# Another order of the seven products in the first two gate/up units, one of them in a down-product bank

## The chip, the cores and the metric

The kernel runs on 1 core of one Trainium2 chip. The metric is the device time of one execution in microseconds (us); where a program runs several times, the median is given. The engines are named as in the profile: PE (TensorE, matmuls), PEld (its weight loads), DVE (VectorE), ACT (ScalarE), POOL (GpSimd), SP (SyncE, which here issues DMA transfers; SPq is its queue).

## What is computed

All in float32; S = 2048 rows, D = 576 columns, F = 4608 hidden columns, 32 heads:

```python
x = A_x
xn = _layernorm(x)
s = _A_ref(xn, ...)                 # attention with a learned feature map
g = _silu((_silu(xn @ w_gate) * (xn @ w_up)) @ w_down)
return x + s * g
```

The change lies in `_silu(xn @ w_gate) * (xn @ w_up)` alone, the gate/up part of the FFN, and in the order in which its inputs are loaded.

## The kernel before

**Precision.** Every float32 operand of a matmul is split in two parts: a high part (ACT, a cast) and the rest (DVE, a subtraction); both stand on lines 58 and 59, in the helper `split`. A product is the sum of three such matmuls per block.

**The FFN in units.** The hidden columns are worked in 36 blocks of 128 (`NF`), and the rows in two halves `i` of 1024. A pair (half, block) is a unit. The first five blocks (`EARLY`) were computed ahead, beside the attention, and are only loaded again in the FFN (`stored`). For the other units `gate_up` makes, from the weights of one block, two tiles of 128 by 512 for gate and two for up, by a scheme with seven products in place of eight (`product`, L702 to L706). A product is seven matmuls of 512 columns: six on the main rows and one on the tail rows (`wt`). The seven are numbered by the weight block that they use, the third argument of `product`: 0 with the input A11, 4 with S1, 1 with A12, 5 with S2, 2 with S3, 6 with A22, 3 with S4. S1 to S4 are sums of input blocks that were stored in DRAM (`sum_dram`); the A blocks are the input itself.

**Banks.** Product results pile up in PSUM. Bank `px` (two copies) takes products 0, 5, 2 and 6 one after the other, and between them ACT copies its state out: to bank `py` after 0 (L747), to `s2` after 5 and to `s3` after 2 (`snap`, L735). Bank `py` takes product 1 on top and gets the silu in place (L751). Bank `pw` takes 4 and 3. DVE adds `pw` to `s3` (L740, `add`), multiplies it with the silu of `px` (L761) to the tile `hb` (L762), and, after product 3, adds `pw` to `s2` and multiplies with `py` to the tile `ha` (L766). The down products have banks of their own, `pd` (two of them, each over two banks of PSUM).

**The weights of a unit.** `gate_up_weights` loads a block (`ld`), POOL makes differences (`ts`, and parts of `ld`, L693 to L696), and ACT and DVE split them into tiles `w` of two blocks each, for products 0 and 1, 4 and 5, 2 and 3, and a single one for 6. There are four of the double tiles and two of the single ones: a new tile takes over one whose products are done. In the first half the split weights are also stored (`w_dram`).

**The down products.** `strassen` queues the products of two pairs of units with the down weights. Its operands are prepared by POOL (differences, L889 to L907), ACT and DVE (splits, tiles `hh` from `ha`, `hb` and `h`, and `dw` from the down weights; the first rows of these lie in `acc`). `fill` takes finished items from the queue and puts their matmuls (L805) between the products of a later unit. The queue is empty during the first two gate/up units; the third is the first that finds something in it. A list scheduler then places every instruction of every engine by its operands and priorities, so a product's matmuls may be placed among those of another unit.

**The order of the loads.** `operands(i)` issues from SP the loads of the inputs of a half in a written order, L650: A11, S1, A12, S2, S3, A22, S4. In the second half all seven are loaded, each into the tile of the first half, so that a load waits for the last product of the first half that reads that tile. The queue of SP is strictly in order.

Of the kernel before, what the change touches and what calls it, by code (L numbers as in the profile page):

```python
# [9 lines left out]
F32 = mybir.dt.float32  # L10
F32R = mybir.dt.float32r
AF = mybir.ActivationFunctionType
# [5 lines left out]
P = 128  # L18
# [4 lines left out]
NF = F // P  # L23
# [6 lines left out]
EARLY = 5  # L30
# [16 lines left out]
def gated_hedgehog_kernel(ctx: ExitStack, tc, x, w_qk, w_v, w_phi, wo, w_gu, w_tail, w_down, ident_in, mask_in, out):  # L47
# [5 lines left out]
    nc = tc.nc  # L53
# [17 lines left out]
    h_dram = dram.tile([2, EARLY, P, HS], F32, name="h_dram")  # L71
# [54 lines left out]
    with ExitStack() as att:  # L126
# [364 lines left out]
        with ExitStack():  # L491
# [5 lines left out]
            for i in range(3):  # L497
                for j in range(4 if i < 2 else 2):
                    w = GROUPS[(4 * i + j) // 2][1]
                    nc.scalar.copy(zc[0:w, 4 * i + j:4 * i + j + 1], kvp[i][0:w, j, w:w + 1])  # L500
            for s in range(2):
                for a, m, name in ((0, 4, ("p2", "vw")[s]), (4, 1, ("vy", "vx")[s])):
                    o, w = GROUPS[a]
                    zp = kps.tile([P, 512], F32, name=name)
# [5 lines left out]
            for i in range(2 * NG):  # L510
                o, w = GROUPS[i // 2]
# [135 lines left out]
    def operands(i):  # L647

        xo = [None] * 7
        for n in (0, 6, 1, 3, 5, 2, 4):  # L650
            if n < 3:
                j = (0, 1, 3)[n]
                if i:
                    t = xpool.tile([P, 5, BT], F32R, name=f"X0{j}")
                    nc.sync.dma_start(t.bitcast(F32), a_dram[n])
                else:
                    t = XB[0][j]
                xo[n] = [t[:, c] for c in range(5)]
                continue
            j = n - 3  # L660
            t = xpool.tile([P, 5, BT], F32R, name=f"X1{j}")
            nc.sync.dma_start(t.bitcast(F32).rearrange("p c n -> p (c n)"),
                              sum_dram[i, :, j].rearrange("p s c n -> p (s c n)"))
            v = t.rearrange("p c n -> p (c n)").rearrange("p (s c n) -> p s c n", s=4, c=5)
            xo[n] = [v[:, :, c] for c in range(5)]
        return xo

    def gate_up_weights(i, f):

        parts, wt = {}, fw.tile([96, 7, P], F32R, name="wt", bufs=2)  # L670
        n, q = divmod(f - EARLY, 4)
        if i == 0:
            ld = fw.tile([P, 2, D], F32, name="ld", bufs=2).rearrange("p a b -> p (a b)")
            ld = ld[:, 0:8 * P].rearrange("p (m c n) -> p m c n", m=4, c=2)
            nc.sync.dma_start(ld, w_gu[f, :, :, 0:2])
            ts = fw.tile([P, D], F32, name="ts")[:, 0:4 * P].rearrange("p (m c n) -> p m c n", m=2, c=2)

        def ready(m, src):
            k = 1 if m == 6 else 2
            w = fw.tile([P, k, 4, P], F32R, name=f"w{k}", bufs=2 if k == 1 else 4)  # L680
            if i:
                nc.sync.dma_start(w.bitcast(F32), w_dram[f - EARLY, :, m:m + k])
            else:
                split(w[:, :, 0:2], w[:, :, 2:4], src)
                if f < NF - 1:
                    nc.sync.dma_start(w_dram[f - EARLY, :, m:m + k], w.bitcast(F32))
            for c in range(k):
                parts[m + c] = w[:, c]

        ready(0, None if i else ld[:, 0:2])  # L690
        nc.sync.dma_start(wt.bitcast(F32), t_dram[n, q].rearrange("b r m n -> (b r) m n"))
        if i == 0:
            nc.gpsimd.tensor_sub(ts[:, 0], ld[:, 2], ld[:, 0])  # L693
            nc.gpsimd.tensor_sub(ts[:, 1], ld[:, 3], ts[:, 0])
            nc.gpsimd.tensor_sub(ld[:, 2], ld[:, 3], ld[:, 2])
            nc.gpsimd.tensor_sub(ld[:, 1], ld[:, 1], ts[:, 1])  # L696
        ready(4, None if i else ts)
        ready(2, None if i else ld[:, 2:4])
        ready(6, None if i else ld[:, 1:2])
        return parts, wt  # L700

    def product(ps, w, m, b, first, last):  # L702
        mm = [(w[0][m][:, i], b[j]) for c in range(2) for i, j in ((c, c), (2 + c, c), (c, 3 + c))]
        mm += [(w[1][:, m], b[2][0:96])]
        for n, (l, r) in enumerate(mm):
            nc.tensor.matmul(ps, l, r, start=first and n == 0, stop=last and n == len(mm) - 1, skip_group_check=True)  # L706

    def short(name, bufs):
        return fq.tile([P, BT], F32, name=name, bufs=bufs)

    def h_tile():
        return [fp.tile([P, BT], F32, name=n, bufs=b) for n, b in (("ha", 7), ("hb", 6))]
# [6 lines left out]
    def stored(src, fill):  # L719
        h = h_tile()  # L720
        for r in range(2):
            nc.sync.dma_start(h[r], src[:, r * BT:(r + 1) * BT])
        for _ in range(2):
            fill()
        return h

    def gate_up(w, xo, fill, opening):
        A11, A12, A22, S2, S4, S3, S1 = xo
        xp, yp, wp = (fps.tile([P, BT], F32, name=n, bufs=b) for n, b in (("px", 2), ("py", 1), ("pw", 1)))
        h = h_tile()  # L730

        def snap(ps):
            t = short("s", 3)
            with tc.high_priority():
                nc.scalar.copy(t, ps)  # L735
            return t

        def add(ps, t):
            with tc.high_priority():
                nc.vector.tensor_add(t, ps, t)  # L740


        if opening:
            nc.tensor.matmul(yp, w[0][0][:, 0], A11[0], start=True, stop=True)
        product(xp, w, 0, A11, True, False)
        with tc.high_priority():
            nc.scalar.copy(yp, xp)  # L747
        product(wp, w, 4, S1, True, False)
        fill()
        product(yp, w, 1, A12, False, True)  # L750
        nc.scalar.activation(yp, yp, AF.Silu)  # L751
        product(xp, w, 5, S2, False, False)
        s2 = snap(xp)
        fill()
        product(xp, w, 2, S3, False, False)
        s3 = snap(xp)
        add(wp, s3)
        fill()
        product(xp, w, 6, A22, False, True)
        with tc.high_priority():  # L760
            nc.scalar.activation(xp, xp, AF.Silu)  # L761
        nc.vector.tensor_mul(h[1], xp, s3)  # L762
        product(wp, w, 3, S4, False, True)
        add(wp, s2)
        with tc.high_priority():
            anchor.append(nc.vector.tensor_mul(h[0], yp, s2))  # L766
        fill()
        return h

# [200 lines left out]
    queue, anchor, share = [], [], [2]  # L970

    def look():
        n = 0
        for step in queue:
            n += step[0]
            if n > 4 or (step is not queue[0] and step[0] == 1 and n > 3):
                break
            if step[1]:
                step[1]()
                step[1] = None  # L980

# [17 lines left out]
    xo = operands(0)  # L999
# [4 lines left out]
    fps = ctx.enter_context(tc.tile_pool(name="fps", bufs=1, space=PSUM, reuse_waits="tile"))  # L1004
    finals, late = {}, list(range(HT))
    for i, n, f in units:
        share[0] = 2 if n < RUSH else 3
        if i == 1 and n == 0:
            xo = operands(1)
        if f >= EARLY:  # L1010
            w = kept.pop() if i and kept else ready.pop(0)
            if (i, f) == (0, NF - 1):
                kept.append(w)
            if todo and (i, f) != (0, NF - 1):
                ready.append(gate_up_weights(*todo.pop(0)))
        h = stored(h_dram[i, f], fill) if f < EARLY else gate_up(w, xo, fill, (i, f) == (0, EARLY))
        if n % 2 == 0:
            g = {"f": (f, units[units.index((i, n, f)) + 1][2]), "h": [h]}
            if n % 4 == 0:
                group = []  # L1020
            if n < NF - 2:
                group.append(g)
        else:
            g["h"].append(h)
        if n >= NF - 2:
            if n % 2:
                plain(i, g["f"], g["h"], finals)
            continue
        if n >= NF - 4 or n % 4 > 1:
            strassen(i, group, n % 2, n < 4)  # L1030
        if n % 2 == 0:
            continue
        if i and n >= 15 and late:
            with tc.issue_after(anchor[-1].ins):
                late_finish(late.pop(0))
        if n == NF - 3:
            for k in range(2):
                queue.insert(len(queue) - 2 + 3 * k,
                             [0, None, [(0, lambda i=i, k=k: combine(i, k, finals))]])
# [37 lines left out]
```

## Time and profile before

| | us |
|---|---|
| median of 3 runs | 1647.71 (1643.01 to 1648.73) |
| profiled execution, its own time | 1645.38 |
| its span in the trace | 1643.6 |
| granted PE clock, mean over the span | 0.998 |
| first product of the first gate/up unit | 512.92 |
| first product of the second half's first gate/up unit | 1065.17 |

Times in the trace count from the start of the span. A timeline row has the start, the length, the engine, the line, the operation, the output and the inputs, the shape and the count, and in brackets the time that the engine stood idle before it with the instruction that ended it. A row of the view of waits has the total, the number of times and the longest. A row of a view by windows has busy time and number of instructions of the engines that it names, then the granted clock, the share of the DMA engines and GB/s. L706 is the line of every product's matmuls, so the output's name (`px`, `py`, `pw`, `pd`) tells them apart.

### The profile page before, as it was taken

How to read it: one execution, taken by the hardware profiler on the slowest of the kernel's cores; microseconds unless marked ns; L12 is line 12 of the kernel's file. 1: busy time of each engine (PE TensorE's matmuls, PEld its weight loads, DVE VectorE, ACT ScalarE, POOL GpSimd, SP SyncE). 2: the span in 40 equal slices, each digit the busy share in tenths (PEclk: the TensorE clock that was granted, in tenths of full speed). 3: DMA queues.
4: the chain of work that ended last, by engine and by line, in shares of the span. 5: the costliest groups of instructions: out<-in, count | busy, mean ns of one | idle time of the engine just before them, and what ended most of it. 6: DMA issues, size and time to landing. Idle time of an engine off the chain costs nothing.

```text
span 1643.6 us, 25222 instructions
## 1 busy us (share of the span) xinstructions
PE 1606.3 (98%) x9385; PEld 1428.2 (87%) x9385; DVE 1173.2 (71%) x1733; ACT 723.1 (44%) x1407; POOL 655.0 (40%) x699
## 2 busy tenths in 40 slices
PE   6999999999999999999999999999999999999997
PEld 5899987999987788888888888888888888888886
DVE  7667768989862678788777788825566766666578
ACT  5533344454432554454444444445433433333334
POOL 3385661433213455355445365313243324133132
PEclk9999999999999999999999999999999999999999
DMA  9522243433239545555545554685454655555445
GB/s 293 197 79 78 88 133 114 119 109 110 79 108 329 183 162 172 182 171 177 174 167 181 178 176 156 222 299 157 134 159 138 199 183 172 168 180 182 139 114 173
DMA packets 121741, 268.47 MB, mean 163 GB/s; under 512 B 12786, under 2 KB 53362, under 8 KB 119826
## 3 DMA queue, kind: packets, MB, share of 16 engines
q1 hardware_dynamic: 106652, 246.49, 45.8%
q0 software_dynamic: 3072, 11.02, 2.5%
q10 hardware_dynamic: 11894, 9.35, 1.8%
q8 instruction: 74, 1.21, 0.3%
q14 instruction: 49, 0.40, 0.1%
HBM read 167.19 MB, written 99.61 MB: 162 GB/s over the span
## 4 chain that ended last, share of the span: by engine, by line
PE 66%; DVE 2%; DMA 1%; issue 1%; POOL 0%; ACT 0%; SPq 0%; DVEq 0%; ACTq 0%
PE pd L805 24%; PE px L706 24%; PE pw L706 12%; PE py L706 6%; PE pe L92 1%; DVE acc L777 0%; DVE w L59 0%; DMA rb<-in_B_w_down 0%; DMA ld<-in_B_w_gu 0%; DVE hh L59 0%; DMA X<-s_dram 0%; DVE dw L59 0%; DVE ha L766 0%; DVE acc L778 0%; DVE s L740 0%
## 5 line engine op out<-in xcount | busy, mean ns | idle before, releaser
L805 PEld LDWEIGHTS pd<-dw,hh 128*128 128x128 f32 x3048 | 433.6, 189 | 25.5 <-DVE dw L59 2.0
L805 PE MATMUL pd<-dw,hh 128*128 128x288 f32 x3048 | 449.7, 297 | 3.2 <-DVE dw L59 1.5
L706 PE MATMUL px<-X,w 128*128 128x512 f32 x1488 | 385.9, 393 | 2.1 <-ACT w L58 1.3
L706 PEld LDWEIGHTS px<-X,w 128*128 128x128 f32 x1488 | 270.2, 188 | 55.5 <-ACT s L735 4.0
L706 PE MATMUL pw<-X,w 128*128 128x512 f32 x744 | 191.8, 393 | 0.0
L706 PEld LDWEIGHTS pw<-X,w 128*128 128x128 f32 x744 | 139.1, 188 | 31.2 <-DVE s L740 0.3
L740 DVE TENSOR_TENSOR s<-pw,s 128x512 f32<-128x512 f32 x124 | 85.3, 688 | 103.2 <-ACT s L735 91.7
L930 DVE TENSOR_TENSOR acc<-pd,acc 128x576 f32<-128x576 f32 x128 | 96.3, 753 | 85.3 <-PE pd L805 85.1
L735 ACT COPY s<-px 128x512 f32<-128x512 f32 x124 | 72.6, 586 | 160.0 <-PE px L706 159.9
L92 PE MATMUL pe<-X,wh 128*128 128x512 f32 (+1 forms) x380 | 121.4, 401 | 5.3 <-ACT h L119 2.2
L58 ACT CAST hh<-ha 128x512 fp32r<-128x512 f32 x140 | 82.7, 619 | 92.9 <-PE pd L805 72.6
L59 DVE TENSOR_TENSOR hh<-ha,hh 128x512 fp32r<-128x512 f32 x140 | 109.9, 811 | 18.1 <-ACT hh L58 17.1
L902 POOL TENSOR_TENSOR hb<-hb 128x512 f32<-128x512 f32 x34 | 46.7, 1372 | 161.9 <-DVE hb L762 161.5
L59 DVE TENSOR_TENSOR w<-ld,w 128x512 fp32r<-128x512 f32 (+1 forms) x93 | 79.6, 858 | 37.6 <-ACT w L58 36.3
L706 PE MATMUL py<-X,w 128*128 128x512 f32 x372 | 97.7, 396 | 1.1 <-ACT py L747 1.1
L706 PE MATMUL px<-X,wt 96*128 96x512 f32 x248 | 97.9, 395 | 0.0
L915 POOL TENSOR_TENSOR ha<-ha 128x512 f32<-128x512 f32 x34 | 52.6, 1563 | 104.0 <-DVE hh L59 104.0
L889 POOL TENSOR_TENSOR h<-ha,hb 128x512 f32<-128x512 f32 x34 | 44.9, 1321 | 123.2 <-DVE ha L766 90.1
L58 ACT CAST w<-ld 128x512 fp32r<-128x512 f32 (+1 forms) x93 | 50.9, 549 | 90.1 <-POOL ld L696 58.0
L92 PEld LDWEIGHTS pe<-X,wh 128*128 128x128 f32 (+1 forms) x380 | 69.9, 189 | 20.6 <-DVE h L122 3.4
L693 POOL TENSOR_TENSOR ts<-ld 128x256 f32<-128x256 f32 x31 | 27.3, 880 | 140.7 <-issue 70.0
L747 ACT COPY py<-px 128x512 f32<-128x512 f32 x62 | 35.5, 572 | 103.7 <-PE px L706 84.4
(262 smaller groups left out, 3238.1 us busy)
## 6 DMA issues: line engine op xcount, KB each, us to landing
w_dram<-w SPq DMA_DIRECT2D x90, 512.0 KB, 2.9
w<-w_dram SPq DMA_DIRECT2D x90, 512.0 KB, 4.5
wt<-t_dram SPq DMA_DIRECT2D x61, 336.0 KB, 3.6
ld<-in_B_w_gu SPq DMA_DIRECT2D x31, 512.0 KB, 4.5
X<-sum_dram SPq DMA_DIRECT2D x8, 1280.0 KB, 11.4
rt<-in_B_w_down SPq DMA_DIRECT2D x33, 288.0 KB, 3.0
rb<-in_B_w_down SPq DMA_DIRECT2D x33, 288.0 KB, 4.3
w_dram<-w SPq DMA_DIRECT2D x30, 256.0 KB, 2.2
```

The source lines that it names most:

```text
L58: nc.scalar.copy(hi, src)
L59: nc.vector.tensor_sub(lo, src, hi)
L92: last = nc.tensor.matmul(ps, l, r, start=n == 0, stop=n == len(pairs) - 1)
L706: nc.tensor.matmul(ps, l, r, start=first and n == 0, stop=last and n == len(mm) - 1, skip_group_check=True)
L735: nc.scalar.copy(t, ps)
L740: nc.vector.tensor_add(t, ps, t)
L747: nc.scalar.copy(yp, xp)
L805: nc.tensor.matmul(ps, l, r, start=first and n == 0 and m == 0, stop=n == len(hs) - 1 and m == 2, skip_group_check=True)
L889: sub(s, g["h"][0][0], g["h"][0][1])
L902: nc.gpsimd.tensor_add(a21, a21, g["h"][1][1])
L915: sub(a12, a12, g["h"][0][0])
L930: nc.vector.tensor_add(a2, pd[:, :, 0:HALF], a2)
```

## The change

In the two first gate/up units of the first half (`opening` 0 and 1) the seven products come in the order 0, 4, 5, 1, 2, 3, 6, all other units keep 0, 4, 1, 5, 2, 6, 3. Product 3 there goes to a bank of the down products (`zp`) and not on top of `pw`, so `s2` gets two additions, of `pw` and of `zp`. The tile `ha` is then made ahead of product 6, and `hb` is the last one. The calls of `fill` are left out in these two units, where the queue is empty. `operands` loads in the order A11, S1, S2, A12, S3, S4, A22, in both halves.

```diff
-        for n in (0, 6, 1, 3, 5, 2, 4):
+        for n in (0, 6, 3, 1, 5, 4, 2):
...
-        if opening:
+        if opening == 0:
             nc.tensor.matmul(yp, w[0][0][:, 0], A11[0], start=True, stop=True)
+
+        def silu_y():
+            nc.scalar.activation(yp, yp, AF.Silu)
+
+        def silu_x(s3):
+            with tc.high_priority():
+                nc.scalar.activation(xp, xp, AF.Silu)
+            nc.vector.tensor_mul(h[1], xp, s3)
+
+        def top(s2):
+            with tc.high_priority():
+                anchor.append(nc.vector.tensor_mul(h[0], yp, s2))
+
         product(xp, w, 0, A11, True, False)
...
         product(wp, w, 4, S1, True, False)
+        if opening < 2:
+            product(xp, w, 5, S2, False, False)
+            s2 = snap(xp)
+            product(yp, w, 1, A12, False, True)
+            silu_y()
+            product(xp, w, 2, S3, False, False)
+            s3 = snap(xp)
+            add(wp, s3)
+            add(wp, s2)
+            zp = fps.tile([P, 2, 512], F32, name="pd", bufs=2)[:, 0]
+            product(zp, w, 3, S4, True, True)
+            add(zp, s2)
+            top(s2)
+            product(xp, w, 6, A22, False, True)
+            silu_x(s3)
+            return h
         fill()
...
-        h = stored(h_dram[i, f], fill) if f < EARLY else gate_up(w, xo, fill, (i, f) == (0, EARLY))
+        h = stored(h_dram[i, f], fill) if f < EARLY else gate_up(w, xo, fill, f - EARLY + (NF if i else 0))
```

What this does to the engines' lists is shown at three places. The first is PE in the first gate/up unit, behind its products 0 and 4. X_61 is A12, X_5302 is S2, X_5304 is S3, X_63 is A22, X_5306 is S4, X_60 is A11; w_5413 and w_5508 are weights of the second and third unit. Before:

```order
L706 MATMUL py<-X_61,w_5380 128x512 x6
L706 MATMUL py<-X_61,wt 128x512
L706 MATMUL px<-X_5302,w_5389 128x512 x6
L706 MATMUL px<-X_5302,wt 128x512
L706 MATMUL px<-X_60,w_5413 128x512 x5
L706 MATMUL px<-X_5304,w_5393 128x512 x6
L706 MATMUL px<-X_5304,wt 128x512
L706 MATMUL px<-X_60,w_5413 128x512
L706 MATMUL px<-X_60,wt 128x512
L706 MATMUL px<-X_63,w_5397 128x512 x6
L706 MATMUL px<-X_63,wt 128x512
L706 MATMUL pw<-X_5306,w_5393 128x512 x6
```

And now:

```order
L706 MATMUL px<-X_5302,w_5389 128x512 x6
L706 MATMUL px<-X_5302,wt 128x512
L706 MATMUL py<-X_61,w_5380 128x512 x6
L706 MATMUL py<-X_61,wt 128x512
L706 MATMUL px<-X_5304,w_5393 128x512 x6
L706 MATMUL px<-X_5304,wt 128x512
L706 MATMUL pd<-X_5306,w_5393 128x512 x6
L706 MATMUL pd<-X_5306,wt 128x512
L706 MATMUL px<-X_63,w_5397 128x512 x6
L706 MATMUL px<-X_63,wt 128x512
L706 MATMUL px<-X_60,w_5413 128x512 x6
L706 MATMUL px<-X_60,wt 128x512
```

The next unit's product 0 is no longer placed in pieces between products 5, 2 and 6, and products on `py` and `pd` stand between those on `px`. On ACT the copy that product 2 needs moves ahead of the silu of `py`, and the copy that opens the second unit (L747, now L760) moves behind the casts of the third unit's weights and the silu of `px`. Before, from the second weight cast on:

```order
L58 CAST w_5422<-ts 128x2x256
L751 ACTIVATE py<-py 128x512
L58 CAST w_5426<-ld 128x2x256
L735 COPY s<-px 128x512
L58 CAST dw<-rt 128x288
L735 COPY s<-px 128x512
L761 ACTIVATE px<-px 128x512
L58 CAST dw<-td 128x288
L58 CAST w_5508<-ld 128x2x256
L58 CAST w_5525<-ld 128x256
L747 COPY py<-px 128x512
```

And now:

```order
L58 CAST w_5422<-ts 128x2x256
L735 COPY s<-px 128x512
L58 CAST w_5426<-ld 128x2x256
L747 ACTIVATE py<-py 128x512
L735 COPY s<-px 128x512
L58 CAST dw<-rt 128x288
L58 CAST w_5510<-ld 128x2x256
L58 CAST w_5527<-ld 128x256
L751 ACTIVATE px<-px 128x512
L58 CAST hh<-ha 128x512
L58 CAST dw<-td 128x288
L760 COPY py<-px 128x512
```

Here the cast of the down difference (`dw<-td`) now stands after the third unit's weight casts and right ahead of the second unit's copy.

The second place is DVE from the second unit's additions to the first splits of the down operands (`hh`, `dw`), and PE's list where the first down products stand. DVE before:

```order
L762 TENSOR_TENSOR hb<-px,s 128x512
L740 TENSOR_TENSOR s<-pw,s 128x512
L59 TENSOR_TENSOR w_5604<-ld,w_5604 128x2x256
L766 TENSOR_TENSOR ha<-py,s 128x512
L59 TENSOR_TENSOR hh<-ha,hh 128x512
L59 TENSOR_TENSOR w_5621<-ld,w_5621 128x256
L59 TENSOR_TENSOR dw<-acc,dw 128x288
```

DVE now:

```order
L59 TENSOR_TENSOR w_5608<-ld,w_5608 128x2x256
L740 TENSOR_TENSOR s<-pd,s 128x512
L756 TENSOR_TENSOR ha<-py,s 128x512
L752 TENSOR_TENSOR hb<-px,s 128x512
L59 TENSOR_TENSOR w_5625<-ld,w_5625 128x256
L59 TENSOR_TENSOR hh<-ha,hh 128x512
L59 TENSOR_TENSOR dw<-acc,dw 128x288
```

The unit's last multiply is now `hb` in place of `ha`, with the same three splits behind it. PE ahead of the first run of down products (L805, now L831), before:

```order
L706 MATMUL pw<-X_5306,w_5426 128x512 x6
L706 MATMUL pw<-X_5306,wt 128x512
L706 MATMUL px<-X_60,w_5604 128x512
L706 MATMUL pw<-X_5300,w_5517 128x512 x6
L706 MATMUL pw<-X_5300,wt 128x512
L706 MATMUL px<-X_60,w_5604 128x512 x2
L706 MATMUL py<-X_61,w_5508 128x512 x3
L805 MATMUL pd<-dw,hh 128x288 x3
```

And now:

```order
L706 MATMUL px<-X_63,w_5430 128x512 x6
L706 MATMUL px<-X_63,wt 128x512
L706 MATMUL px<-X_60,w_5510 128x512 x6
L706 MATMUL px<-X_60,wt 128x512
L706 MATMUL pw<-X_5300,w_5519 128x512 x6
L706 MATMUL pw<-X_5300,wt 128x512
L831 MATMUL pd<-dw,hh 128x288 x4
L706 MATMUL py<-X_61,w_5510 128x512 x2
```

Three matmuls of the third unit's product 1 and three of the fourth unit's product 0 no longer stand ahead of this run. The third place is SP at the start of the second half, the loads of its seven inputs; `a_dram` holds A11, A12 and A22 in this order, `sum_dram` the sums. Before:

```order
L655 DMA X_10746<-a_dram 128x2560
L662 DMA X_10748<-sum_dram 128x2560
L655 DMA X_10750<-a_dram 128x2560
L662 DMA X_10752<-sum_dram 128x2560
L662 DMA X_10754<-sum_dram 128x2560
L655 DMA X_10756<-a_dram 128x2560
L662 DMA X_10758<-sum_dram 128x2560
```

And now:

```order
L655 DMA X_10750<-a_dram 128x2560
L662 DMA X_10752<-sum_dram 128x2560
L662 DMA X_10754<-sum_dram 128x2560
L655 DMA X_10756<-a_dram 128x2560
L662 DMA X_10758<-sum_dram 128x2560
L662 DMA X_10760<-sum_dram 128x2560
L655 DMA X_10762<-a_dram 128x2560
```

S2 is loaded ahead of A12, and S4 ahead of A22. The products of the first unit there follow it, though the code's order for that unit is the old one: 0, 4, 5, 1, 2, 3, 6.

More of the change, by code (lines that the diff above doesn't have):

```diff
@@ L748, in gate_up @@
         product(wp, w, 4, S1, True, False)
+        if opening < 2:
[14 more added lines that the diff above has]
+            return h
         fill()
         product(yp, w, 1, A12, False, True)
-        nc.scalar.activation(yp, yp, AF.Silu)
+        silu_y()
         product(xp, w, 5, S2, False, False)
@@ L759, in gate_up @@
         product(xp, w, 6, A22, False, True)
-        with tc.high_priority():
-            nc.scalar.activation(xp, xp, AF.Silu)
-        nc.vector.tensor_mul(h[1], xp, s3)
+        silu_x(s3)
         product(wp, w, 3, S4, False, True)
         add(wp, s2)
-        with tc.high_priority():
-            anchor.append(nc.vector.tensor_mul(h[0], yp, s2))
+        top(s2)
         fill()
```

## The prediction

> **What bounds the kernel now.** I read the page first: engine shares, then the chain that ended last.
>
> ```profile
> span 1643.6 us, 25222 instructions
> PE 1606.3 (98%) x9385; PEld 1428.2 (87%) x9385; DVE 1173.2 (71%) x1733; ACT 723.1 (44%) x1407; POOL 655.0 (40%) x699
> PE 66%; DVE 2%; DMA 1%; issue 1%; POOL 0%; ACT 0%; SPq 0%; DVEq 0%; ACTq 0%
> ```
>
> TensorE is busy 98% of the span, and of the chain's named work nearly all is its own. So only two things can move the end: matmul work, which the change leaves as it is, and moments in which PE waits. I therefore read the stages (columns: window, length, PE busy with matmul records, granted clock, DMA share, GB/s).
>
> ```profile
> 600.00:700.00 100.00, 100.00 (x561) 1.00 0.52 176
> 512.68:546.69 34.01, 29.90 (x122) 1.00 0.79 266
> ```
>
> In the steady FFN PE never waits; in the opening, where the first two gate/up units run, 4.1 us of 34.0 are empty. Who PE waits for there, from the view of waits between 512 and 580 us:
>
> ```profile
> PE pd L805 <- DVE dw L59: 1.5, 1, 1.5
> PE px L706 <- ACT w L58: 1.3, 2, 0.8
> PE px L706 <- ACT s L735: 0.7, 2, 0.5
> PE py L706 <- ACT py L747: 0.4, 1, 0.4
> ```
>
> The timeline of PE shows where (start, length, what, idle before):
>
> ```profile
> 512.92 1.54 PE L706 MATMUL px<-X,w 128*128 128x512 f32 x6
> 514.53 1.54 PE L706 MATMUL pw<-X,w 128*128 128x512 f32 x6
> ...
> 523.06 1.65 PE L706 MATMUL px<-X,w 128*128 128x512 f32 x6 [0.20 <-ACT s L735]
> ...
> 527.37 0.50 PE L706 MATMUL px<-X,w 128*128 128x512 f32 x1 [0.82 <-ACT w L58]
> ...
> 530.43 1.66 PE L706 MATMUL py<-X,w 128*128 128x512 f32 x6 [0.44 <-ACT py L747]
> ...
> 537.50 1.66 PE L706 MATMUL px<-X,w 128*128 128x512 f32 x6 [0.54 <-ACT s L735]
> ...
> 541.52 0.50 PE L706 MATMUL px<-X,w 128*128 128x512 f32 x1 [0.52 <-ACT w L58]
> ...
> 544.18 0.97 PE L706 MATMUL py<-X,w 128*128 128x512 f32 x3
> 546.69 0.89 PE L805 MATMUL pd<-dw,hh 128*128 128x288 f32 x3 [1.54 <-DVE dw L59]
> ```
>
> One product is seven matmuls (six here, one on the tail rows) and takes 514.53 - 512.92 = 1.61 us, so 0.230 us a matmul. From 512.68 to 546.69 the timeline holds 119 matmuls of width 512 (2 x 49 + 1 for the first two units, 17 of the third, 3 of the fourth) and 2 narrow ones of the down products (about 0.13 us each): 119 x 0.230 + 0.3 = 27.7 us. The stretch lasts 34.0, so **6.3 us** are lost in all; this is more than the 4.1 shown as idle, since a stall also costs the restart of the stream. The last wait, for the split of the down weights (I call it **the gate**), costs 546.69 - (544.18 + 3 x 0.23) = 1.8. The waits inside the two units cost the other **4.5**. And right behind the gate the granted clock falls:
>
> ```profile
> 545.00:546.00 1.00, 0.15 (x1) 1.00 0.00 0
> 547.00:548.00 1.00, 1.00 (x5) 0.50 0.00 0
> 550.00:551.00 1.00, 1.00 (x6) 0.82 0.00 0
> ```
>
> That is about 3.4 us at half speed (from 547 to 550.4), so 1.7 us of work lost. All that the opening holds is 6.3 + 1.7 = 8.0 us, 0.49% of the time.
>
> **The change, part by part.** Matmuls, copies and adds are the same in number; the bank of the seventh product is a down-product bank that no item uses yet. I number products as the code's third argument does: before 0, 4, 1, 5, 2, 6, 3; now 0, 4, 5, 1, 2, 3, 6.
>
> *Inside the two units.* Products 0, 5, 2 and 6 all add into one bank, with a copy by ScalarE between them. Before, 5, 2 and 6 followed each other, so PE either stood still for the copy (0.20 and 0.54 above) or was given parts of the next unit's product 0, which waited for weights (0.82, 0.52). Now 1 lies between 5 and 2, and 3 between 2 and 6: each copy has 1.61 us of other matmuls over it.
>
> ```profile
> 514.73 0.57 ACT L747 COPY py<-px 128x512 f32<-128x512 f32 x1 [4.52 <-PE px L706]
> 517.72 0.62 ACT L58 CAST w<-ts 128x512 fp32r<-128x512 f32 x1 [1.75 <-PE py L706]
> 519.86 0.58 ACT L735 COPY s<-px 128x512 f32<-128x512 f32 x1
> 526.36 0.43 ACT L58 CAST dw<-td 128x288 fp32r<-128x288 f32 x1 [0.75 <-POOL td L890]
> ```
>
> Stepping PE at 1.61 us from 512.92: product 5 starts at 516.14, and the copy that it needs ends at 515.3. Product 2 starts at 519.37; ahead of its copy stands one cast of weights, which takes over a buffer that product 5 frees, so it runs at 517.8 to 518.4 and the copy to 518.9: in time. Product 6 starts at 522.6, its copy ends at 521.8. The second unit's product 0 starts at 524.2 with its weights long split, product 4 at 525.8. Its product 5 is due at 527.4 and needs ScalarE's copy behind the cast of the down difference; that cast waits for GpSimd and a load, as the last row shows, until 526.4, so the copy ends near 527.3. This is the closest place; a slip costs what it slips. Then 1 at 529.1, 2 at 530.7, 3 at 532.3, 6 at 533.9, all with 0.4 us or more in hand. The units end at 535.5, and the third's products 0 and 4 bring PE to the gate at 512.92 + 16 x 1.614 = **538.75**. The term is -4.5 us, bounded by 0 (every wait comes back elsewhere) and -4.5 (there is no more).
>
> *The gate.* PE comes sooner; when does it open? These rows are VectorE's and GpSimd's before it:
>
> ```profile
> 540.04 0.69 DVE L762 TENSOR_TENSOR hb<-px,s 128x512 f32<-128x512 f32 x1 [1.87 <-ACT px L761]
> ...
> 542.24 0.69 DVE L766 TENSOR_TENSOR ha<-py,s 128x512 f32<-128x512 f32 x1
> 542.84 0.92 DVE L59 TENSOR_TENSOR hh<-ha,hh 128x512 fp32r<-128x512 f32 x1
> 543.68 1.51 DVE L59 TENSOR_TENSOR w<-ld,w 128x256 fp32r<-128x256 f32 x1
> 545.12 1.52 DVE L59 TENSOR_TENSOR dw<-acc,dw 128x288 fp32r<-128x288 f32 x1
> ```
> ```profile
> 543.16 1.75 POOL L889 TENSOR_TENSOR h<-ha,hb 128x512 f32<-128x512 f32 x1
> 544.87 1.45 POOL L907 TENSOR_TENSOR ha<-hb,ha 128x512 f32<-128x512 f32 x1
> ```
>
> From the end of the unit's last multiply (ha, 542.93) to the end of the down weights' split (546.64) there are three VectorE instructions and 3.7 us; two take 1.5 us beside GpSimd. In the new order the same three (the order of two exchanged) stand behind the last multiply, which is now hb. It waits for product 6 (535.5), the cast of a spare weight block and the activation on ScalarE: about 537.2 to 537.9. The gate opens at 537.9 + 3.7 = **541.6**. PE waits from its two free down matmuls (0.3 us after 538.75) to 541.6, 2.6 instead of 1.8: a term of **+0.8**. Bounds: no wait at all (-1.8), or up to the point where the whole gain is eaten (+4.5).
>
> *Behind the gate.* The half clock came after an empty 1.5 us; with 2.6 empty I take it to come again: **0**, bounded by -1.7 if it doesn't. The Trainium skill, "TensorE: Matmul & The Clock Gate", section "What's actually happening", has the drop only after an idle window of about 3.4 us. This trace disagrees: 1.5 us of idle, and the clock is 0.50; that page's rule would leave the clock alone in the new kernel, which is the second rival below.
>
> *The second half's loads.* The list of loads is used there too: S2 now goes third, ahead of A12, and A22 last. A load waits for its buffer's last reader, and A12 now queues behind S2, which product 5 releases.
>
> ```profile
> 1056.19 0.32 SPq L655 DMA_DIRECT2D X<-a_dram  x1
> 1057.81 2.88 SPq L662 DMA_DIRECT2D X<-sum_dram  x2
> 1068.41 1.54 PE L706 MATMUL py<-X,w 128*128 128x512 f32 x6
> 1073.38 1.53 PE L706 MATMUL px<-X,w 128*128 128x512 f32 x6
> ```
> ```profile
> X<-sum_dram SPq DMA_DIRECT2D x1, 1280.0 KB, 11.1
> ```
> ```profile
> 1057.00:1058.00 1.00, 1.00 (x7) 0.88 (x6) 1.00 (x1) 0.19 (x1) 0.16 (x1) 1.00 1.07 451
> ```
>
> The third load goes out at 1057.81 instead of 1056.19, and the order has its product third as well, at 1068.41. As the fourth load, S2 landed 11.1 us after its issue (the middle fence, for the first of the two at 1057.81), at 1068.9. If it took that from its issue whatever lies ahead, PE would wait 0.5 us. But the transfers are full at 451 GB/s in that very microsecond, and 1.31 MB takes 2.9 us of it, so with one tile less ahead it lands near 1066. A12 then lands at 1068.9 for a product at 1073.4. Term: **0**, bounds 0 and +0.5; behind it products 3 and 6 only swap.
>
> **Sum**, against the profiled execution: -4.5 + 0.8 + 0 + 0 = **-3.7 us**, from 1645.4 (span 1643.6 and 1.8 around it) to 1641.7. That execution lies 2.3 below the median of 1647.7, so the median forecast is 1647.7 - 3.7 = **1644.0**, with 1642 to 1646 as its own range (a gate at 539.6 to 543.6).
>
> **The rivals.**
>
> 1. *The gate holds.* What PE saves, it waits for there: the time of the down operands is set by VectorE and GpSimd (the 1.5 us rows), not by PE. Time 1647.7. For it: the longest wait of the opening is exactly this one. Against: its chain starts at the unit's last multiply, which itself waits for PE (1.87 idle before hb).
>
> 2. *The clock stays.* The wait at the gate leaves the clock at 1.00, and the 1.7 us of half speed go too: -3.7 - 1.7 = -5.4, 1642.3. For it: the waits of 0.4 to 0.8 us before left the clock at 1.00, so a drop doesn't follow every wait:
>
> ```profile
> 520.00:530.00 10.00, 8.96 (x37) 1.00 1.01 332
> 530.00:540.00 10.00, 9.03 (x38) 1.00 0.77 263
> ```
>
> Against: 1.5 was enough for one, and this wait is longer. (The rule of the page named above speaks for this rival.)
>
> 3. *Nothing is left.* The gate is open when PE comes, all 8.0 us go: 1639.7. Against: the three VectorE instructions can't begin before product 6 ends.
>
> 4. *Slower.* More VectorE splits fall beside GpSimd's differences. The split of 288 columns is 1.52 there, the one of 256 columns 1.51, against 0.92 for the wider one that only partly met it. Beside the gate's three, six or so splits and multiplies lie between 529 and 538; at 0.6 to 0.8 more each the gate moves by 3.6 to 4.8. It decides from a gate at 546.69 - 6 x 0.23 = 545.3 (the six gate/up matmuls that PE has not done by then), 3.7 after mine. At 1.1 past it, with a second stretch of half clock (1.7) for a wait of over 7 us: +2.8, 1650.5.
>
> That the change doesn't do what it says can be set aside: the listed order shows the seven products as written.
>
> **How the numbers follow.** Forecast 0.50; gate holds 0.17; clock stays 0.20; nothing left 0.05; slower 0.08. The range leaves out the third rival and the end of the fourth, and allows for the scatter of the three runs (1643.0 to 1648.7): 1640.5 to 1649.0. About 0.5%, 8.2 us, is what a measurement of this kernel can tell from no change. Even all 8.0 us of the opening stay under it, so faster by more than that has 0.05 (scatter on top of the third rival), slower by more 0.03, within it 0.92.
>
> **What would show it.** In the new profile: no wait above 0.2 us for the copies L735 and L760 or for weights before the first down product; that product reached near 538.8 and started near 541.6, released by a split of dw; a window of clock 0.50 of 3.4 us behind it; no PE idle between 1065 and 1090. I am wrong if PE waits in the second unit's product 5 for over 0.5 us, if the gate is past 544, or if the down products behind it wait again and again.

## The result, and the profile after

The changed kernel takes **1640.12 us**, the median of 13 runs (1637.25 to 1642.29); the kernel before takes 1644.44 in 13 runs taken alongside (1642.56 to 1648.73). The ratio of the two is 0.9971, with a 95% interval from 0.9962 to 0.998: by it the change saves 4.8 us, between 3.3 and 6.2 (the two medians lie 4.3 apart). The forecast was a saving of 3.7 us. That size lies in the interval; the forecast time of 1644.0 and its lower end of 1640.5 do not cover 1640.12, and the section on the prediction says which step did that.

The head of the profile after shows the same amount of matmul work in a shorter span (1643.6 before):

```profile
span 1638.7 us, 25220 instructions
PE 1604.5 (98%) x9385; PEld 1429.4 (87%) x9385; DVE 1175.5 (72%) x1735; ACT 723.8 (44%) x1407; POOL 655.3 (40%) x699
```

PE has the same 9385 matmuls, and ScalarE the same 1407 instructions. VectorE has two more (1735 in place of 1733): in each of the two units `s2` gets a second addition, where the prediction had the adds the same in number. The 34 us from the opening matmul on and the 30 behind them, by windows (window, length, PE busy with matmul records, granted clock, DMA share, GB/s), and a stretch of the second half's first unit:

```profile
513.50:547.50 34.00, 31.87 (x144) 1.00 0.78 266
547.50:577.50 30.00, 29.83 (x169) 1.00 0.61 209
1065.00:1090.00 25.00, 25.00 (x145) 1.00 0.95 334
```

In its first 34 us PE is busy for 31.9 and gets 144 matmul records done, in place of 29.9 and 122. The clock is at 1.00 behind them too. In the stretch of the second half PE has no gap. What PE waited for, between 505 and 580 us:

```profile
PE pd L831 <- DVE dw L59: 2.1, 2, 1.2
PE px L706 <- ACT s L735: 0.2, 1, 0.2
```

Four rows have become two. The waits for weights and for the copy of L747 (now L760) are gone, and of the 0.7 for the copies of L735 there is 0.2 left, behind the gate at 549.00. What is left ahead of that is the gate, now in two pieces. The timeline of PE (start, length, what, idle before) shows both:

```profile
513.50 0.40 PE L744 MATMUL py<-X,w 128*128 128x512 f32 x1
513.73 1.54 PE L706 MATMUL px<-X,w 128*128 128x512 f32 x6
...
521.80 1.54 PE L706 MATMUL pd<-X,w 128*128 128x512 f32 x6
...
539.53 0.30 PE L831 MATMUL pd<-dw,hh 128*128 128x288 f32 x1
541.01 0.66 PE L831 MATMUL pd<-dw,hh 128*128 128x288 f32 x3 [1.18 <-DVE dw L59]
541.51 0.62 PE L706 MATMUL py<-X,w 128*128 128x512 f32 x2
543.07 1.33 PE L831 MATMUL pd<-dw,hh 128*128 128x288 f32 x8 [0.94 <-DVE dw L59]
```

The row at 521.80 is product 3 in the free bank. Between the opening matmul at 513.50 and the first down product at 539.53 no row has a wait in brackets: sixteen products go by in 26.03 us, so 113 matmuls at 0.230. At the gate, from start to start: 541.01 - 539.53 less one narrow matmul (0.13) is 1.35, and 543.07 - 541.51 less two wide ones (0.46) is 1.10; together **2.45 us** lost, 1.8 before. The timeline of VectorE tells what the two pieces wait for:

```profile
537.88 0.69 DVE L752 TENSOR_TENSOR hb<-px,s 128x512 f32<-128x512 f32 x1 [0.51 <-ACT px L751]
538.49 0.42 DVE L59 TENSOR_TENSOR w<-ld,w 128x256 fp32r<-128x256 f32 x1
538.82 1.76 DVE L59 TENSOR_TENSOR hh<-ha,hh 128x512 fp32r<-128x512 f32 x1
540.51 0.45 DVE L59 TENSOR_TENSOR dw<-acc,dw 128x288 fp32r<-128x288 f32 x1
540.88 1.77 DVE L59 TENSOR_TENSOR hh<-ha,hh 128x512 fp32r<-128x512 f32 x1
542.57 0.45 DVE L59 TENSOR_TENSOR dw<-rt,dw 128x288 fp32r<-128x288 f32 x1
542.94 0.68 DVE L59 TENSOR_TENSOR hh<-h,hh 128x512 fp32r<-128x512 f32 x1
```

GpSimd's rows of that time are these:

```profile
538.65 1.39 POOL L915 TENSOR_TENSOR h<-ha,hb 128x512 f32<-128x512 f32 x1 [1.73 <-DVE hb L752]
540.67 1.43 POOL L933 TENSOR_TENSOR ha<-hb,ha 128x512 f32<-128x512 f32 x1 [0.63 <-DVE hh L59]
544.07 1.19 POOL L923 TENSOR_TENSOR td<-td,acc 128x288 f32<-128x288 f32 x1 [1.97 <-DVE dw L59]
```

The split of `dw<-acc` ends at 540.96 and lets the three matmuls at 541.01 go; the one of `dw<-rt` ends at 543.02 and lets the eight at 543.07 go. Each has a split of `hh` of some 1.76 us ahead of it, and beside each of these stands one of GpSimd's differences; the split of `hh` at 542.94, with GpSimd idle, took 0.68.

Which of the two begins first makes the difference. Both long splits (538.82, 540.88) begin while a difference is running, and end 0.54 and 0.55 us behind its end (540.04, 542.10). The splits at 538.49 and 540.51 begin 0.16 us ahead of one, and take no longer than without it. The whole trace of before bears this out for the splits of `hh`: 158 with no difference of GpSimd beside them took 0.68 to 0.69 us; 25 that began ahead of one took 0.68 to 0.69 too; and of the 63 that began while one was running, 57 took 0.72 or more, and all 57 ended 0.55 us behind it.

Both profiled executions can now be laid side by side, from the opening matmul to the first product of the second half:

| | before | after |
|---|---|---|
| opening matmul | 512.68 | 513.50 |
| from there to the second half's first product | 552.49 | 546.50 |
| from there to the last long run of down products | 556.93 | 557.06 |

So 6.0 us come out of the middle stretch and 0.8 go back ahead of it, where the two kernels are the same. That stretch (I call it **the middle**) is the measure of the experiments below: it leaves out the scatter of what runs ahead of it.

One part of the 6.0 lies far from the change. Outside the opening, one row of before, in the first half at 826 us, has no counterpart in after:

```profile
823.98 1.76 PE L805 MATMUL pd<-dw,hh 128*128 128x288 f32 x12
826.35 1.65 PE L706 MATMUL py<-X,w 128*128 128x512 f32 x6 [0.61 <-ACT py L747]
```

```profile
819.72 1.76 PE L831 MATMUL pd<-dw,hh 128*128 128x288 f32 x12
821.33 1.53 PE L706 MATMUL py<-X,w 128*128 128x512 f32 x6
```

From the down products to the next product it is 2.37 us before and 1.61 after: **0.76** saved. ScalarE's copy was late there, since the weight cast ahead of it waited for GpSimd, and GpSimd for a load of down rows. ScalarE before:

```profile
825.41 0.41 ACT L58 CAST w<-ld 128x256 fp32r<-128x256 f32 x1 [5.67 <-POOL ld L696]
825.72 0.58 ACT L747 COPY py<-px 128x512 f32<-128x512 f32 x1
```

GpSimd before, and after:

```profile
820.54 0.81 POOL L890 TENSOR_TENSOR td<-rb,rt 128x288 f32<-128x288 f32 x1 [1.16 <-DMA rb<-in_B_w_down]
```

```profile
815.08 1.02 POOL L916 TENSOR_TENSOR td<-rb,rt 128x288 f32<-128x288 f32 x1
```

The load itself goes out at 815.09 before and at 810.84 after, 4.25 earlier, as PE does there (4.26); but it had landed for a start at 815.08, at most 4.2 us after its issue, and before it let GpSimd start only at 820.54, after 5.4.

### The profile page after: what moved, and what is told of

Its sections match the earlier page's. It is cut to its first block, busy times and chain, and to the rows that moved or that the text cites. A ratio compares the mean times of both kernels' runs of the same rounds, so it can differ in the third digit from the quotient of the medians.

```text
span 1638.7 us, 25220 instructions
## 1 busy us (share of the span) xinstructions
PE 1604.5 (98%) x9385; PEld 1429.4 (87%) x9385; DVE 1175.5 (72%) x1735; ACT 723.8 (44%) x1407; POOL 655.3 (40%) x699
## 4 chain that ended last, share of the span: by engine, by line
PE 90%; DVE 3%; DMA 3%; POOL 1%; issue 1%; ACT 1%; SPq 0%; ACTq 0%; POOLq 0%; DVEq 0%
PE px L706 24%; PE pd L831 24%; PE pw L706 12%; PE py L706 6%; PE p L92 6%; PE pe L92 5%; PE p L614 4%; PE po L594 2%; PE kvp L295 2%; PE vx L383 1%; PE pt L588 1%; PE vw L383 1%; DMA sraw<-in_A_w_v 1%; DMA xn<-in_A_x 1%; DMA x_dram<-xr 1%
## 5 line engine op out<-in xcount | busy, mean ns | idle before, releaser
L831 PEld LDWEIGHTS pd<-dw,hh 128*128 128x128 f32 x3048 | 432.4, 188 | 26.2 <-DVE dw L59 2.9
L831 PE MATMUL pd<-dw,hh 128*128 128x288 f32 x3048 | 448.5, 297 | 3.8 <-DVE dw L59 2.1
L735 ACT COPY s<-px 128x512 f32<-128x512 f32 x124 | 72.6, 585 | 158.3 <-PE px L706 158.3
L760 ACT COPY py<-px 128x512 f32<-128x512 f32 x62 | 35.5, 572 | 102.3 <-PE px L706 84.8
```

The lines of the kernel that those rows point to most:

```text
L831: nc.tensor.matmul(ps, l, r, start=first and n == 0 and m == 0, stop=n == len(hs) - 1 and m == 2, skip_group_check=True)
```

## The experiments

All ratios are to the kernel before, run on the same chip. "The middle" is the time from the opening matmul (L744) to the first product of the second half's first gate/up unit.

**The kernels themselves once more.** One more profile of each, for the middle and for the clock behind the gate.

> The kernel before, a second profile, for the clock behind the gate. Theory (the drop depends on where the 1.5 us wait falls in the clock's own time, since one of two profiles with that wait and the old product order shows it and one does not): the same wait of 1.5 us, and the drop may be there or not; the stretch from the first gate/up matmul to the second half's first product is 552.5 us with it, 550.8 to 551.2 without. Rival (the drop belongs to the kernel): 0.50 for 3.4 us right behind the gate again.

> The changed kernel, a second profile. Theory: the two waits of 1.2 and 0.9 us at the gate again and no drop of the clock there, the stretch 546.5 us. Rival (the clock may drop here as well): 548.2 us with 0.50 for 3.4 us behind the gate.

Before again: 1642.33 us, the middle 511.38 to 1062.55, **551.17**. The gate is the same, but the granted clock behind it stays at 1.00. The row of the timeline and a window:

```profile
545.34 0.66 PE L805 MATMUL pd<-dw,hh 128*128 128x288 f32 x3 [1.53 <-DVE dw L59]
```

```profile
547.00:548.00 1.00, 1.00 (x8) 1.00 0.00 0
```

So the half clock that the prediction read as a part of the kernel is a part of one execution. It made the middle 552.49 - 551.17 = 1.3 us longer, somewhat less than the 1.7 that 3.4 us at half speed came to. After again: 1638.12 us, the middle 510.71 to 1058.12, **547.41**. It has the two pieces of the gate (1.09 and 0.93), and a wait at the place that the prediction called the closest, the second unit's product 5:

```profile
526.05 1.67 PE L706 MATMUL px<-X,w 128*128 128x512 f32 x6 [0.43 <-ACT py L760]
```

With it, and with 0.16 for a copy of L735, the first down product is reached at 537.68, 26.97 after the opening matmul in place of 26.03: this is the 0.9 between 547.41 and 546.50. The place is as tight as was said, since the copy came in time in one profile and not in the other. What it was held up by is another cast than the one that the prediction named: ScalarE stood still ahead of the cast of the third unit's single weight block, here for 2.19 us and in after for 1.64, and then went through its queue to the copy without a stop.

```profile
523.76 0.41 ACT L58 CAST w<-ld 128x256 fp32r<-128x256 f32 x1 [2.19 <-POOL ld L696]
```

Every version below has one profile. The middle repeated to 0.01 us in the kernel before, without a drop of the clock, but not closer than 0.9 in the changed one, so differences below 1 us between versions with the new order are not told apart by it.

**The new order of the loads alone.**

```diff
 before, with
-        for n in (0, 6, 1, 3, 5, 2, 4):
+        for n in (0, 6, 3, 1, 5, 4, 2):
```

> The kernel before with the new order of the loads alone (S2 ahead of A12, S4 ahead of A22); the products as before. Theory (the gain is PE's waits inside the two units, and nothing else): no change, 0 within 1.5 us, and the stretch from the first gate/up matmul to the second half's first product stays at 552 to 553 us (before 552.5, with 1.7 of half clock in it; 550.8 if the clock stays full). Rival (the loads matter, since the second half's first unit now has its products in another order): a gain of 1.5 us or more, seen behind the second half's first product.

Measured: 1644.47 us, ratio 1.0002 (0.9994 to 1.0011), the middle 551.18, the same four rows of waits (1.5, 1.5, 0.8 and 0.5). Here too the gate's wait is 1.52 and the clock behind it 1.00. The new order of the loads shows no cost and no gain.

**The change with the old order of the loads.**

```diff
 after, with
-        for n in (0, 6, 3, 1, 5, 4, 2):
+        for n in (0, 6, 1, 3, 5, 2, 4):
```

> The change with the old order of the loads. Theory: as fast as the change (4 to 5 us below before), since all four sums of the first half have landed before they are read and the second half's loads are limited by what the transfers carry. Rival (the new order of the loads is needed so that product 5 or 3 does not wait for its input): 1 us or more of the gain is gone, with PE idle ahead of product 5 of the first unit.

Measured: 1640.08 us, ratio 0.9972 (0.9961 to 0.9984), the middle **546.58**, the same two rows of waits as the change, with the same numbers. So the saving comes from the products' order with its bank, and none of it from the loads.

**The new products' order in the first unit alone.**

```diff
 after, with
-        if opening < 2:
+        if opening < 1:
```

> The change with the new order in the first gate/up unit alone; the second unit is as before. Theory: the waits of the first unit and of its border go (0.4, 1.0 and 0.6 us start to start), those of the second stay (0.7 and 0.7), and the gate's chain starts at ha again, as before: 2.0 to 2.5 us less than before, a wait for the copy into s (L735) ahead of the second unit's product 6. Rival (the gain is the gate, which opens sooner because hb ends the second unit): no gain, 0 within 1 us.

Measured: 1640.78 us, ratio 0.9976 (0.9965 to 0.9987), the middle 547.99, so 3.2 saved of 551.18. The waits between 505 and 580 us:

```profile
PE pd L831 <- DVE dw L59: 1.5, 1, 1.5
PE px L706 <- ACT w L58: 0.5, 1, 0.5
```

The first unit has all its waits taken away and the second keeps its 0.5 for weights; the expected wait for the copy into `s` there did not come. The gate is the old one in one piece, with the clock at 1.00 behind it. The wait at 826 us is there too (0.61, at 822.60 in this kernel). So by the middles the first unit carries some two thirds of 4.7, the second the rest together with the wait at 826; the ratios of the runs (0.9976 here, 0.9971 for the change) do not tell the two kernels apart. The gate is split only where the second unit has the new order too.

**The new order without the free bank.** Product 3 goes on top of `pw` again, so it needs VectorE's addition first and is put last.

```diff
 after, with
             add(wp, s3)
-            add(wp, s2)
-            zp = fps.tile([P, 2, 512], F32, name="pd", bufs=2)[:, 0]
-            product(zp, w, 3, S4, True, True)
-            add(zp, s2)
-            top(s2)
             product(xp, w, 6, A22, False, True)
             silu_x(s3)
+            product(wp, w, 3, S4, False, True)
+            add(wp, s2)
+            top(s2)
             return h
```

> The change without the bank of the down products: in the two units 0, 4, 5, 1, 2, 6, 3, with product 3 on pw as before. Theory: one copy (after 5) is covered, the other (after 2) is not, so each unit waits 0.6 to 0.8 us ahead of product 6 or gets pieces of the next unit there; the gate's chain starts at ha, later: 2 to 3 us less than before in place of 4 to 5. Rival (exchanging 1 and 5 is all that matters): the whole gain stays, within 1 us of the change.

Measured: 1643.96 us, ratio 0.9991 (0.9982 to 1.0), the middle 550.95. This profile has the half clock behind the gate (1.54 us of wait); with the 1.3 of that taken off, the middle is 549.65, so 1.5 saved in place of 4.7. The place was not the expected one. Ahead of product 6 nothing waits, since the scheduler puts parts of the next unit's product 0 there; but the second unit's product 5 then waits for ScalarE:

```profile
531.27 1.66 PE L706 MATMUL px<-X,w 128*128 128x512 f32 x6 [1.97 <-ACT py L760]
```

```profile
527.55 0.44 ACT L58 CAST dw<-td 128x288 fp32r<-128x288 f32 x1 [0.74 <-POOL td L914]
530.32 0.41 ACT L58 CAST w<-ld 128x256 fp32r<-128x256 f32 x1 [2.33 <-POOL ld L696]
530.63 0.58 ACT L760 COPY py<-px 128x512 f32<-128x512 f32 x1
```

The copy (530.63) is queued behind a cast of weights that waits 2.33 us for GpSimd. So by the middles two thirds of the saving hang on the free bank and on the place that it allows product 3.

**The gate taken away, in before and in the change.** A rule in `strassen`'s preparation holds the first down operands back until a unit's last multiply has been issued (the last one in program order at that point, `anchor[-1]`). The experiment drops it:

```diff
 before, and after, with
-                with tc.issue_after(anchor[-1].ins) if first and i == 0 and part == 0 else ExitStack():
+                with ExitStack():
```

> The kernel before with the same rule taken off. Theory: the 1.8 us at the gate shrink to below 0.7, and with them the drop to half clock (1.7 us) that followed in the first profile: 1 to 3 us less than before. Rival (the early splits get in the way of the units' own splits and copies): no gain or a loss, with longer waits for weights (L58) and copies (L747, L735) inside the two units.

> The change, with the rule taken off that holds the first down operands' preparation behind the second unit's last multiply of py (issue_after): VectorE now splits the down weights (dw) among the two units' own work, and only the splits of hh stay behind them. Theory (the two waits of 1.2 and 0.9 us at the first down products, 2.4 us start to start, are VectorE's queue of splits): 1.0 to 2.0 us less than the change, so a ratio to before of 0.996, with at most one wait there, for hh. Rival (the waits come from GpSimd's differences or from ha and hb themselves): as fast as the change, 0 within 0.7 us, the waits still 2 us in all.

Before without the rule: 1641.6 us, ratio 0.998 (0.9971 to 0.9989), the middle 549.65, so 1.5 saved. No wait at the gate is left in the view, and most of the others stay (1.4 for weights, 0.5 and 0.2 for copies, 0.3 new for VectorE's addition to `s`). The change without the rule: 1638.37 us, ratio 0.996 (0.9947 to 0.9972), the middle 546.05, so by the middles 0.5 to 1.4 below the two profiles of the change, where 1 to 2 were expected. Its waits:

```profile
PE px L706 <- ACT s L735: 1.4, 1, 1.4
PE pd L831 <- DVE hh L59: 0.6, 1, 0.6
```

At the gate 0.6 is left, but a new wait of 1.4 stands in the second unit. The timelines of ScalarE and of GpSimd show why:

```profile
531.24 0.43 ACT L58 CAST dw<-td 128x288 fp32r<-128x288 f32 x1 [3.44 <-POOL td L923]
531.58 0.61 ACT L58 CAST w<-ts 128x512 fp32r<-128x512 f32 x1
532.10 0.58 ACT L735 COPY s<-px 128x512 f32<-128x512 f32 x1
```

```profile
527.84 1.13 POOL L922 TENSOR_TENSOR td<-rb,rt 128x288 f32<-128x288 f32 x1
528.94 1.50 POOL L915 TENSOR_TENSOR h<-ha,hb 128x512 f32<-128x512 f32 x1
530.40 0.81 POOL L923 TENSOR_TENSOR td<-td,rb 128x288 f32<-128x288 f32 x1
```

GpSimd makes `h`, an operand of the second item, 1.5 us long ahead of `td`; ScalarE's queue stands still for that `td`, and the copy that PE needs is behind it.

**The rule taken off for the first item alone.** The reading just given says how to keep the gain: only the splits of the first item (p1) go early, the second (p7), with `h`, is still held back.

```diff
 after, with
-                with tc.issue_after(anchor[-1].ins) if first and i == 0 and part == 0 else ExitStack():
+                with tc.issue_after(anchor[-1].ins) if first and i == 0 and f is p7 else ExitStack():
```

> The change, with the rule that holds the first down operands back until the unit's last multiply taken off for the first item (p1) alone and kept for the second (p7), so that GpSimd's difference h of the first pair is not made early and does not stand ahead of the down differences that ScalarE's queue waits for. My theory (the gate is the three VectorE splits behind the last multiply, and the 1.45 us wait of the experiment early_split came from GpSimd's early h alone): PE has no wait above 0.5 us in the two units; at the gate only one split of hh stands behind hb, so the wait there is 0.6 instead of 2.45 us in all, and the stretch from the opening matmul to the second half's first product is 544.7 (between 544 and 545.5); time ratio to before near 0.996 (1638 us). Rival (the splits that go early come back as waits of the weights or copies in the second unit, whichever they are): 1 us or more of waits inside the second unit and a stretch of 546 or more, as with early_split.

Measured: **1636.27 us** (1635.71 to 1638.09), ratio 0.9951 (0.9938 to 0.9965), the middle **544.64**. Its median is the lowest and its middle the shortest of all versions, though its interval still meets those of the change and of the version without the rule. One row of waits is left between 505 and 580 us, and the timeline shows that there is a single piece:

```profile
PE pd L831 <- DVE hh L59: 0.8, 1, 0.8
```

```profile
540.29 0.83 PE L831 MATMUL pd<-dw,hh 128*128 128x288 f32 x5
541.91 1.23 PE L831 MATMUL pd<-dw,hh 128*128 128x288 f32 x7 [0.79 <-DVE hh L59]
```

From start to start the gate now loses 541.91 - 540.29 - 5 x 0.13 = 1.0 us in place of 2.45, and the middle is 1.9 shorter than in the change's first profile. The middle came within 0.1 of what was expected, with the wait at 0.8 in place of 0.6. This bears out both points: the gate is the row of VectorE splits behind the unit's last multiply, and the 1.4 of the version without the rule came from GpSimd's early `h`.

## Why the prediction was wrong, and where it was right

**The step that failed is the last one of the sum**: "That execution lies 2.3 below the median of 1647.7, so the median forecast is 1647.7 - 3.7 = 1644.0". The median of three runs was taken as the kernel's time. Two of those three were high: 13 runs put it at 1644.44, and the later sets at 1644.83 (24 runs), 1644.54 (15) and 1643.88 (9). The same sum from 1644.44 gives 1640.7, and the sum against the profiled execution gave 1641.7; the measured time is 1640.12. Of the 3.9 us by which the forecast lies too high, the anchor makes 3.3, and the size of the saving (4.3 between the medians, not 3.7) the other 0.6. The scatter was seen (1643.0 to 1648.7), but the lower end left it only 3.5 us; the lowest of the three alone asked for 1643.0 - 3.7 = 1639.3.

A part of the scatter goes with the clock. In eleven profiles the opening matmul starts anywhere from 510.71 to 514.24 us, though the attention ahead of it is the same program. In the five in which it comes after 513, stretches of half clock lie ahead of it, and in four of the six others there is none. But those four still start from 510.71 to 512.88, and of the 48 later runs of the kernel before, those with a mean clock of 0.999 average 1644.2 and those with 0.997 average 1645.3, while the 23 with 0.998 run from 1641.9 to 1647.2. So most of the scatter has no cause shown here. One of the stretches of half clock, in the profile after, at 19 to 22 us:

```profile
19.00:20.00 1.00, 1.00 (x8) 0.60 0.06 24
20.00:21.00 1.00, 1.00 (x7) 0.50 0.57 55
21.00:22.00 1.00, 1.00 (x6) 0.50 0.69 217
```

**Inside the two units: -4.5, right.** The 4.5 us are gone: the first down product is reached 26.03 us after the opening matmul, forecast 538.75 - 512.68 = 26.07. The second unit's product 5 was named as the closest place; it came in time in after, and waited 0.43 in the second profile, where the first down product came 26.97 after the opening matmul, so that 0.9 of the 4.5 came back.

**The gate: +0.8, right in size, not in its make.** It loses 2.45 us in place of 2.6, so +0.65. The three instructions from the last multiply on take 540.96 - 538.57 = 2.4 us, not the 3.7 taken from before: the splits of `w` and `dw` now begin just ahead of GpSimd's differences (0.42 and 0.45, before 1.51 and 1.52), while that of `hh` begins behind the start of one (1.76, before 0.92). The gate so opens at 541.01 in this trace, 27.5 after the opening matmul, forecast 28.9. What was missed is a second piece: the next item's `hh` and `dw` behind it, on which PE stands still again for 0.94.

**Behind the gate: 0, wrong as a statement, small as a sum.** The half clock does not come with the kernel. Of the five profiles with a wait of 1.5 us at the gate (before, before again, the loads alone, the first unit alone, no free bank) it follows in two, before and no free bank; in the three profiles of the change and of the change with the old loads, with two waits of about 1.2 and 0.9, it does not come. What it costs is 1.3, by the two profiles of before. The rival "the clock stays" had the time right for this pair of profiles (-5.4 forecast, span -4.9), but priced as if the drop were in every run of before. At two in five it is worth 0.5 us in a mean, an estimate from five profiles. The Trainium skill, "TensorE: Matmul & The Clock Gate", section "What's actually happening", gives a drop after an idle window of about 3.4 us, and says that the window runs freely, so that transitions depend on where in it the work falls. The length agrees (some 3.4 us at 0.50); the condition does not, since PE was empty for 1.5 us and no more. A window that runs freely explains a part of it. In each trace the clock changes only on a grid with steps of 3.41 us (before: 546.95, 550.36 and 1639.21, 1 and 320 steps). All eleven drops ahead of the end of these profiles follow a step that holds at least 1.5 us without matmuls, and a wait that a border of the grid cuts in two brought none: in the first unit alone the 1.52 are cut into 0.57 and 0.95, in no free bank the 1.97 into 0.51 and 1.46. But in before again and the loads alone the 1.5 us lie within one step and no drop follows; what decides there stays open.

**The second half's loads: 0, right.** The loads alone: ratio 1.0002, and after has no wait of PE from 1059 to 1095.

**What the sum did not hold: the wait at 826 us, -0.76.** "In the steady FFN PE never waits" was read from one window, 600 to 700 us, and taken for the 480 us between the opening and the second half. In the six profiles in which the second unit has the old order or no free bank it is there (0.6 or 0.7), in the five others it is not. Its chain is shown above: a load of down rows lands at least 1.2 us later, with the same issue beside the same work. Why it lands later stays open; no run here tells it.

So the sum without any half clock comes to -4.5 + 0.65 - 0.76 = -4.6, and the middle went from 551.17 to 546.50, -4.7. The interval of the runs is 3.3 to 6.2. The rival "the gate holds" fell: its price was the whole gain, and the gate took 0.65. "Slower" fell with it: VectorE's splits beside GpSimd did stretch (1.76), but two of the three then began ahead of GpSimd's differences and were not. Within 0.5%, at 0.92, is what came.

## What to carry to other kernels

Work out what a change saves in the stage where it acts, and measure it there, between two events that bracket the stage; the median of three runs is no anchor to a microsecond where runs scatter by more than five, and a range must hold the error of the anchor as well as that of the sum. When products are reordered to cover copies, look at the in-order queue of the engine that copies: the longer waits for copies that came back here (1.97, 1.4, 0.43) were all for a copy queued behind a cast whose input GpSimd had not finished. The free bank, with the place for a product that it opens, was worth two thirds of the gain, and a rule that holds operands back for one item too many some 2 us more.

## What was not expected of the hardware

The granted clock fell to 0.50 for some 3.4 us after PE had been empty for 1.5 us, but in two profiles of five with the same wait, so a drop in one profile is no property of a kernel. A VectorE split of 128 by 512 took 0.68 us alone or when it began ahead of a GpSimd subtraction, and up to 1.77 at the gate when it began while one was running; one of 288 columns took 0.45 and 1.52. So which of the two began first decided what the gate cost, not how many splits there were. And the landing of one load (5.4 us from its issue, or 4.2 at most), some 270 us behind the two units, or the wait that it causes, went with the second unit's order and bank in all eleven profiles.
